# Attention's head mixings as float32 products in quarters of TensorE's array, two groups at once

## The chip, the cores and the metric

The kernel runs on one core of a Trainium2 chip. The metric is the device time of one execution in microseconds; before the change it is 1365.61 us, the median of three runs (1364.88 to 1365.74). Engines are named as in the profile: PE is the tensor engine (PEld its weight loads), DVE the vector engine, ACT the scalar engine, POOL GpSimd, SP the engine that issues most DMA transfers.

## The reference

```python
# q, k, v: (4, 12, 448, 64); w_pre, w_post: (12, 12)
scores = scale * np.matmul(q, k.transpose(0, 1, 3, 2))
scores = np.einsum('bhij,hg->bgij', scores, w_pre)      # premix over heads
scores = scores - np.max(scores, axis=-1, keepdims=True)
attn = np.exp(scores)
attn = attn / (np.sum(attn, axis=-1, keepdims=True) + 1e-09)
attn = np.einsum('bhij,hg->bgij', attn, w_post)          # postmix over heads
x = np.matmul(attn, v)                                   # then (1792, 768)
x = (sigmoid(x @ w_gate) * (x @ w_val)) @ w_out          # d_ff 1536
h = x @ w_in                                             # d_ff 2048
out = (h * sigmoid(1.702 * h)) @ w_out2                  # all in float32
```

Attention mixes its 12 heads twice with a 12 x 12 matrix: the scores before the softmax, and the weights after it.

## The kernel before, in words

The first part of the program is attention, the rest are the two feed-forward networks (class `Ffn`). A few of the feed-forward weights are loaded and prepared beside attention, and the feed-forward part's first matmuls (`pg`, L1005) stand among attention's last ones.

A unit is a batch and up to 120 query rows: 120, 120, 120 and 88 rows a batch, 16 units. For a unit, `qk` (L245) multiplies q and k for two heads at once, one on array rows 0 to 63 and one on rows 64 to 127, in three float32r passes over parts that were split high and low; `qk_out` copies the scores from PSUM to `sc`, with 120 query rows on partitions and head by column on the free axis. `relayout` (L266) moves ten of these rows by one DMA on SP into a tile `gt` whose partitions are (row, head), 10 x 12 = 120 of them. That is a group; there are 180. Then come, for each group,

- `split_hi` and `split_lo` (L214 and L278 in the trace): the scores are split into a high and a low float32r part, the cast on ACT or DVE, the subtraction on POOL or DVE;
- `premix` (L285): three float32r passes of 448 columns by a 120 x 120 block-diagonal weight, itself split (`wphl`), into one PSUM bank;
- `rowmax` (L292, DVE), `expo` (L299, ACT, which also sums each row);
- `norm` (L307, L309 on DVE, L312 on ACT): one over the sum, and the block-diagonal `wpost` scaled by it into `w2`;
- `postmix` (L330): four plain float32 matmuls whose stationary side is 112 columns of exp and whose moving side is `w2`, so the result comes out with keys on partitions; the trace counts two passes for each float32 matmul;
- `post_out` (L214, to `at`): the copy out of PSUM, on ACT or DVE.

When a unit's groups are through, `av` (L349) multiplies `at` by v, two heads at once on the two column halves of the array, and `av_out` and `store` bring it to DRAM.

The order of all this on each engine is made when the program is built, by `Work`: every piece has a due time (a group every `STEP` = 2350), a cost on each engine that may run it, what it needs, and which buffers it takes and gives back. `order()` picks piece by piece the one that can begin first. PSUM stands there as two pools: four single banks `s` (for transposes of the first batch, premix, postmix, A·V) and two double banks `q` (q·k, and later transposes). Engines run their lists strictly in that order.

## Time and profile before

| | us |
|---|---|
| median of three runs | 1365.61 |
| span of the profiled execution | 1370.6 |
| PE busy over the span | 1342.6 (98%) |
| DVE busy | 1097.7 (80%) |
| ACT busy | 913.1 (67%) |
| POOL busy | 173.7 (13%) |

The profiled execution's own time is its span. Busy time of PE counts each pass from its start to its modelled end, and passes overlap, so a busy PE need not issue at its peak; how far apart passes start is read from runs of equal passes. POOL works only in the first 12 of the profile's 40 slices, which is attention.

### The profile page before, as it was taken

How to read it: one execution, taken by the hardware profiler on the slowest of the kernel's cores; microseconds unless marked ns; L12 is line 12 of the kernel's file. 1: busy time of each engine (PE TensorE's matmuls, PEld its weight loads, DVE VectorE, ACT ScalarE, POOL GpSimd, SP SyncE). 2: the span in 40 equal slices, each digit the busy share in tenths (PEclk: the TensorE clock that was granted, in tenths of full speed). 3: DMA queues.
4: the chain of work that ended last, by engine and by line, in shares of the span. 5: the costliest groups of instructions: out<-in, count | busy, mean ns of one | idle time of the engine just before them, and what ended most of it. 6: DMA issues, size and time to landing. Idle time of an engine off the chain costs nothing.

```text
span 1370.6 us, 26095 instructions
## 1 busy us (share of the span) xinstructions
PE 1342.6 (98%) x8862; PEld 1230.6 (90%) x8862; DVE 1097.7 (80%) x2534; ACT 913.1 (67%) x2162; POOL 173.7 (13%) x160
## 2 busy tenths in 40 slices
PE   7999999999999999999999999999999999999998
PEld 5888888888888999998999889998999998999998
DVE  5888878898889889989988988877875697665763
ACT  5888978888888756776765766565666364565442
POOL 2443433344442000000000000000000000000000
PEclk9999999999999999999999999999999999999999
DMA  5655755744455665557997645586752875214644
GB/s 148 193 163 163 225 168 155 224 159 159 158 180 182 224 220 162 172 177 251 309 306 265 209 158 170 195 278 224 232 166 82 251 245 175 69 41 141 208 141 136
DMA packets 224148, 256.40 MB, mean 187 GB/s; under 512 B 70268, under 2 KB 211472, under 8 KB 224016
## 3 DMA queue, kind: packets, MB, share of 16 engines
q1 hardware_dynamic: 222992, 254.50, 58.3%
q8 instruction: 70, 1.15, 0.4%
q14 instruction: 62, 0.51, 0.1%
q10 hardware_dynamic: 960, 0.23, 0.1%
q0 software_dynamic: 64, 0.01, 0.0%
HBM read 160.18 MB, written 55.97 MB: 158 GB/s over the span
## 4 chain that ended last, share of the span: by engine, by line
PE 46%; DVE 7%; DMA 5%; issue 2%; ACT 2%; SPq 0%; DVEq 0%; ACTq 0%
PE pq L1060 25%; PE po L1547 15%; PE py L1005 5%; DMA ws<-in_moe_w_in_dram 3%; DVE w L927 2%; DMA sb<-xy 1%; DVE xy L1042 1%; DVE wc L802 1%; DVE s L1198 1%; DVE wc L804 1%; DVE wc L801 1%; DVE s L1069 1%; DMA xy<-kept 0%; DMA kept<-wc 0%; ACT xy L1041 0%
## 5 line engine op out<-in xcount | busy, mean ns | idle before, releaser
L1060 PE MATMUL pq<-xy,w 128*128 128x448 f32 x2394 | 482.7, 363 | 3.9 <-ACT w L921 1.0
L1060 PEld LDWEIGHTS pq<-xy,w 128*128 128x128 f32 x2394 | 447.9, 188 | 38.1 <-ACT w L921 2.6
L1547 PE MATMUL po<-wf,xy 128*128 128x384 f32 x1176 | 208.5, 338 | 3.1 <-ACT xy L993 1.6
L1547 PEld LDWEIGHTS po<-wf,xy 128*128 128x128 f32 x1176 | 207.6, 188 | 3.8 <-ACT xy L993 1.9
L278 POOL TENSOR_TENSOR ghl<-gt,ghl 120x448 fp32r<-120x448 f32 (+1 forms) x144 | 168.9, 1179 | 243.1 <-ACT ghl L214 176.9
L330 PEld LDWEIGHTS pso<-w,ex 120*112 120x112 f32 (+1 forms) x1440 | 160.3, 177 | 22.6 <-ACT ex L299 6.9
L330 PE MATMUL pso<-w,ex 120*112 120x120 f32 (+1 forms) x1440 | 173.3, 270 | 3.3 <-ACT ex L299 1.5
L1005 PE MATMUL py<-xy,w 128*128 128x448 f32 x864 | 173.7, 362 | 1.5 <-DVE xy L991 1.4
L1005 PEld LDWEIGHTS py<-xy,w 128*128 128x128 f32 x864 | 162.0, 188 | 12.8 <-DVE xy L991 2.1
L285 PE MATMUL psp<-ghl,wphl 120*120 120x448 f32 x540 | 141.8, 388 | 1.9 <-ACT ex L299 1.4
L1041 ACT CAST xy<-xy 128x384 fp32r<-128x384 f32 (+2 forms) x212 | 89.2, 457 | 59.3 <-DVE xy L1198 56.3
L292 DVE TENSOR_REDUCE st<-psp 120x1 f32<-120x448 f32 x180 | 108.8, 613 | 13.6 <-PE psp L285 13.4
L299 ACT ACTIVATE ex<-psp,st 120x448 f32<-120x448 f32 x180 | 113.6, 635 | 7.3 <-DVE st L292 2.8
L1042 DVE TENSOR_TENSOR xy<-xy 128x384 fp32r<-128x384 f32 (+2 forms) x212 | 95.9, 487 | 23.4 <-ACT xy L1041 23.3
L285 PEld LDWEIGHTS psp<-ghl,wphl 120*120 120x120 f32 x540 | 89.5, 184 | 17.4 <-ACT ex L299 3.9
L1198 DVE TENSOR_TENSOR xy<-xy 128x384 f32<-128x384 f32 (+2 forms) x184 | 91.0, 512 | 16.9 <-DMA xy<-xd 7.4
L921 ACT CAST w<-xy 128x384 fp32r<-128x384 f32 x110 | 55.2, 511 | 53.9 <-DVE xy L1198 32.1
L214 ACT CAST ghl<-gt 120x448 fp32r<-120x448 f32 (+1 forms) x135 | 75.7, 566 | 17.3 <-PE psp L285 12.0
L927 DVE TENSOR_TENSOR w<-wt,w 128x384 fp32r<-128x384 f32 x108 | 59.3, 554 | 27.7 <-ACT w L921 27.6
L798 ACT ACTIVATE wc<-ws 128x384 f32<-128x384 f32 x108 | 59.8, 554 | 32.2 <-DMA ws<-in_moe_w_in_dram 23.2
L245 PE MATMUL psq<-kq 64*120 64x448 f32 (+1 forms) x576 | 75.1, 392 | 3.7 <-ACT sc L214 3.1
L349 PEld LDWEIGHTS psv<-at,vt 112*64 112x64 f32 x1536 | 73.7, 137 | 5.2 <-issue 1.3
(96 smaller groups left out, 1793.1 us busy)
## 6 DMA issues: line engine op xcount, KB each, us to landing
gt<-sc SPq DMA_DIRECT2D x172, 210.0 KB
wf<-sb SPq DMA_DIRECT2D x64, 384.0 KB
xy<-kept SPq DMA_DIRECT2D x60, 384.0 KB
ws<-in_moe_w_out_dram SPq DMA_DIRECT2D x56, 384.0 KB
kept<-wc SPq DMA_DIRECT2D x108, 192.0 KB
ws<-kept SPq DMA_DIRECT2D x46, 384.0 KB
sb<-xy SPq DMA_DIRECT2D x32, 384.0 KB
ws<-in_moe_w_in_dram SPq DMA_DIRECT2D x32, 384.0 KB
```

Source lines behind the costliest of these rows:

```text
L278: eng.tensor_tensor(out=t[:m, 1], in0=gt.pop(s)[:m], in1=t[:m, 0].bitcast(F32), op=ALU.subtract)
L285: nc.tensor.matmul(ps[:m, :S], wphl[:m, wp, :m], t[:m, gp], start=(i == 0), stop=(i == 2))
L292: nc.vector.tensor_reduce(out=st[:m, 0:1], in_=pre[s][:m, :S], axis=AX.X, op=ALU.max, negate=True)
L299: nc.scalar.activation(t[:m], pre.pop(s)[:m, :S], AF.Exp, bias=st[:m, 0:1], scale=1.0, accum_out=st[:m, 1:2])
L330: nc.tensor.matmul(ps[:JC, c, :, :n], e[:m, c * JC:(c + 1) * JC], w[:m, :, :n], start=True, stop=True)
L927: self.nc.vector.tensor_tensor(out=w[:, 1], in0=self.source(i), in1=w[:, 0].bitcast(F32), op=ALU.subtract)
L1005: self.nc.tensor.matmul(acc[hb][:, :self.S], st, act[k0 + kc][hb][:, ap], start=(k0 + kc == 0 and part == 0 and ap == 0), stop=(k0 + kc == ...
L1041: self.nc.scalar.copy(dst[:, 0], src)
L1042: self.after(n, lambda: self.nc.vector.tensor_tensor(out=dst[:, 1], in0=src, in1=dst[:, 0].bitcast(F32), op=ALU.subtract))
L1060: nc.tensor.matmul(x, st, A[p][c][:, ap], start=(first and c + part + ap == 0), stop=(c == self.KG - 1 and part == 1), skip_group_check=no ...
L1198: self.nc.vector.tensor_tensor(out=dst, in0=x, in1=y, op=op)
L1547: nc.tensor.matmul(acc[:, :PW], x[:, part], w[:, wp], start=(start and part == 0 and wp == 0), stop=(stop and part == 1), skip_group_check ...
```

## The change

The heads are mixed in quarters of the array. A group now holds four blocks of five (or four) rows: 5 x 12 = 60 partitions fit one half of the array, and two blocks lie on partitions 4 to 63 and 64 to 123 of `gts`, two more beside them on the free axis. `premix` is four plain float32 matmuls of 64 x 64 by 448 columns, one in each quarter, into two banks (one for each row half). `postmix` is 32 float32 matmuls: for each of four key chunks and two blocks on the free axis, two column halves of keys (64 and 48) by two row halves. A unit of 120 rows has six such groups, one of 88 rows five (two of 20 rows, three of 16): 92 in all. The scores are no longer split, so `split_hi`, `split_lo` and `split_w` are gone, and the premix waits for the two DMAs of its group directly. Scaling `w2` moves from ACT to POOL, for both blocks at once. `rowmax`, `expo` and `post_out` run twice a group. The score buffers `gts` are five fixed tiles whose first 32 partitions POOL clears once; `build_w` builds each weight in two halves.

PSUM is now eight single banks which `Work` hands out by number: a piece asks for `banks`, and each copy out `frees` one. Four of them (`kept`) outlive attention; pieces marked `late` (the last unit's) use those alone. `STEP` is 3600, and buffers for exp and `w2` are five of the double size instead of eight. The due times of the feed-forward weights prepared beside attention are multiplied by 0.72.

```diff
-    IG = 10
-    CI = 12 * IG
+    IG = 5
+    CI = 120
+    NR = IG * H
...
-    SL = 2
-    EB = 8
+    EB = 5
...
-        ps_s = ctx.enter_context(tc.tile_pool(name="ps_s", bufs=SB, space=PSUM))
-        ps_q = early.enter_context(tc.tile_pool(name="ps_q", bufs=2, space=PSUM, side="right"))
-
-        wphl = const.tile([CI, 2, CI], F32R, name="wphl")
-        wpre = const.tile([CI, CI], F32, name="wpre")
-        wpost = const.tile([CI, H, IG], F32, name="wpost")
+        bank = [pool.enter_context(tc.tile_pool(name=f"bank{i}", bufs=1, space=PSUM, side=side)).tile([128, 512], F32, name=f"bank{i}")
+                for pool, side, some in ((ctx, "left", range(SB)), (early, "right", range(SB, 8))) for i in some]
+        now = {}
...
+        wpre = const.tile([128, 64], F32, name="wpre")
+        wpost = const.tile([128, H, IG], F32, name="wpost")
+        gts = [const.tile([128, 2, S], F32, name=f"gt{i}") for i in range(PF + 1)]
...
+            for x in (wpre, wpost, *(x[:32] for x in gts)):
+                nc.gpsimd.memset(x, 0.0)
...
+                for half in range(2):
+                    off = 64 - NR if (i, half) == (0, 0) else 0
+                    p0 = 64 * half + off
+                    nc.gpsimd.dma_start(rep[p0:p0 + NR], src.unsqueeze(0).broadcast_to([IG, H, H]))
...
-        def relayout(s):
-            u, g, count, m = groups[s]
-            t = g_p.tile([CI, S], F32, tag="g", name="gt")
-            nc.sync.dma_start(t[:m * H], sc[u][g:g + (m - 1) * count + 1:count])
-            gt[s] = t
-
-        def split_hi(s, eng):
-            m = groups[s][3] * H
-            t = g_p.tile([CI, 2, S], F32R, tag="ghl", name="ghl", bufs=SL + 1)
-            copy(eng, t[:m, 0], gt[s][:m])
-            ghl[s] = t
-
-        def split_lo(s, eng):
-            m = groups[s][3] * H
-            t = ghl[s]
-            eng.tensor_tensor(out=t[:m, 1], in0=gt.pop(s)[:m], in1=t[:m, 0].bitcast(F32), op=ALU.subtract)
+        def relayout(s, j):
+
+            u, g, r0, x, count, m = groups[s]
+            r0 += x + j
+            nc.sync.dma_start(gts[s % len(gts)][64 - m * H:64 + m * H, j], sc[u][r0:r0 + (2 * m - 1) * count + 1:count])
 
         def premix(s):
-            m = groups[s][3] * H
-            ps = ps_s.tile([128, 512], F32, tag="s", name="psp")
-            t = ghl.pop(s)
-            for i, (wp, gp) in enumerate(((0, 0), (1, 0), (0, 1))):
...
+            m = groups[s][-1]
+            x = gts[s % len(gts)]
+            pre[s] = banks_of(now["x"])
+            for col in range(2):
+                for row, r in enumerate((slice(0, 64), slice(64, 64 + m * H))):
+                    nc.tensor.matmul(pre[s][row][64 * col:64 * col + 64, :S], wpre[r], x[r, col], start=True, stop=True,
+                                     tile_position=(64 * row, 64 * col))
+
...
+        def expo(s, j):
+            if j == 0:
+                ex[s] = e_p.tile([128, 2, S], F32, tag="e", name="ex")
             st = rs[s]
-            nc.scalar.activation(t[:m], pre.pop(s)[:m, :S], AF.Exp, bias=st[:m, 0:1], scale=1.0,
-                                 accum_out=st[:m, 1:2])
-            ex[s] = t
+            nc.scalar.activation(ex[s][:, j], pre[s][j][:, :S], AF.Exp, bias=st[:, j:j + 1], scale=1.0,
+                                 accum_out=st[:, 2 + j:3 + j])
+            if j:
+                del pre[s]
...
-                w2[s] = w2_p.tile([CI, H, IG], F32, tag="w2", name="w2")
-                nc.scalar.activation(w2[s][:m], wpost[:m], AF.Copy, scale=r)
+                w2[s] = w2_p.tile([128, 2, NR], F32, tag="w2", name="w2")
+                nc.gpsimd.tensor_tensor(out=w2[s], in0=wpost.rearrange("p g i -> p (g i)").unsqueeze(1).broadcast_to([128, 2, NR]),
+                                        in1=r.unsqueeze(2).broadcast_to([128, 2, NR]), op=ALU.mult)
...
         def postmix(s):
-            u, g, count, n = groups[s]
-            m = n * H
+
+            u, m = groups[s][0], groups[s][-1]
             if u not in at:
                 at[u] = a_p.tile([JC, NJ, H, CI], F32, tag="a", name="at")
-            ps = ps_s.tile([128, NJ, H, IG], F32, tag="s", name="pso")
+            ps = [x[:, :NJ * H * 2 * IG].rearrange("p (c g i) -> p c g i", c=NJ, g=H) for x in banks_of(now["x"])]
             e = ex.pop(s)
-            w = w2.pop(s)
+            w = w2.pop(s).rearrange("p j (g i) -> p j g i", g=H)
             for c in range(NJ):
-                nc.tensor.matmul(ps[:JC, c, :, :n], e[:m, c * JC:(c + 1) * JC], w[:m, :, :n],
-                                 start=True, stop=True)
+                for j in range(2):
+                    i0 = IG - m if j == 0 else 0
+                    for k in (slice(0, 64), slice(64, JC)):
+                        for row in range(2):
+                            r = slice(64 * row, 64 * row + (i0 + m) * H)
+                            nc.tensor.matmul(ps[row][k, c, :, j * m:(j + 1) * m], e[r, j, c * JC + k.start:c * JC + k.stop],
+                                             w[r, j, :, i0:i0 + m], start=True, stop=True, tile_position=(64 * row, k.start))
...
+            re = []
+            for j in range(2):
+                re.append(work.add(t - PF * STEP + j, dict(SP=(820, 5000 if s < PF else 3500)), lambda e, j=j: relayout(s, j),
+                                   needs=made[u], takes=() if j else ("g",), behind=re[:1]))
+            moved.setdefault(u, []).extend(re)
+            pm = work.add(t, dict(PE=(800, 970)), lambda e: premix(s), needs=re, banks=2, late=s >= TAIL, gives=("g",), mode="quad")
+            xs = []
+            for j in range(2):
+                mx = work.add(t + 1000 + 600 * j, dict(DVE=(530, 615)), lambda e, j=j: rowmax(s, j), needs=[pm],
+                              takes=() if j else ("st",), behind=xs[:1])
+                xp = work.add(t + 1700 + 800 * j, dict(ACT=(830, 920)), lambda e, j=j: expo(s, j), needs=[mx],
+                              takes=() if j else ("e",), frees=((pm, j),), behind=xs[1:])
+                xs = [mx, xp]
+            n0 = work.add(t + 3500, dict(DVE=(75, 190)), lambda e: norm(s, 0), needs=xs[1:])
+            n1 = work.add(t + 3600, dict(DVE=(80, 190)), lambda e: norm(s, 1), needs=[n0])
+            n2 = work.add(t + 3700, dict(POOL=(450, 800)), lambda e: norm(s, 2), needs=[n1], takes=("w2",), gives=("st",))
+            po = work.add(t + 5400, dict(PE=(1000, 1170)), lambda e: postmix(s), needs=[n2],
+                          takes=("a",) if g == 0 else (), banks=2, late=s >= TAIL, gives=("e", "w2"), mode="quad")
...
```

On PE, in the middle of attention, a stretch of the list before reads (`psp` is a premix, `pso` a postmix, `psq` q·k; a matmul's result stands left of the arrow; x3 is three in a row):

```order
L330 MATMUL pso_4095<-w2_4021,ex_4002 112x120 x4
L330 MATMUL pso_4107<-w2_4036,ex_4026 112x120 x4
L285 MATMUL psp_4115<-ghl_3942,wphl_255 120x448 x3
L330 MATMUL pso_4122<-w2_4076,ex_4058 112x120 x4
L285 MATMUL psp_4135<-ghl_4009,wphl_255 120x448 x3
L285 MATMUL psp_4142<-ghl_4051,wphl_255 120x448 x3
L285 MATMUL psp_4152<-ghl_4127,wphl_255 120x448 x3
L245 MATMUL psq_4167<-kq_1838 120x448 x6
L245 MATMUL psq_4174<-kq_2859 120x448 x6
```

and after, from one premix to the start of the next postmix:

```order
L302 MATMUL bank6_273<-gt0_280,wpre_278 64x448
L302 MATMUL bank4_265<-gt0_280,wpre_278 64x448
L302 MATMUL bank6_273<-gt0_280,wpre_278 64x448
L302 MATMUL bank4_265<-gt0_280,wpre_278 64x448
L239 MATMUL bank3_261<-ident_285,nat_2074 128x112 x4
L239 MATMUL bank1_253<-ident_285,nat_2074 128x112 x4
L351 MATMUL bank0_249<-w2_3241,ex_3224 64x12x5
L351 MATMUL bank2_257<-w2_3241,ex_3224 64x12x5
L351 MATMUL bank0_249<-w2_3241,ex_3224 48x12x5
L351 MATMUL bank2_257<-w2_3241,ex_3224 48x12x5
L351 MATMUL bank0_249<-w2_3241,ex_3224 64x12x5
L351 MATMUL bank2_257<-w2_3241,ex_3224 64x12x5
```

A group's premix has gone from three passes of the whole array into one bank to four quarter matmuls that alternate between two banks; the postmix that begins at the end goes on for 32 matmuls, alternating between its two banks and between 64 and 48 keys.

On ACT, a stretch of the list before (`ghl` is the high part of the split scores, `w2` the scaled weight, `ex` exp, `at` the postmix's copy out, `sc` that of q·k):

```order
L312 ACTIVATE w2_2967<-wpost_257,st_2911 120x120
L299 ACTIVATE ex_2970,st_2955<-psp_2930,st_2955 120x448
L214 COPY at_2739<-pso_2959 112x48x10
L299 ACTIVATE ex_2995,st_2972<-psp_2937,st_2972 120x448
L299 ACTIVATE ex_3000,st_2993<-psp_2948,st_2993 120x448
L312 ACTIVATE w2_3013<-wpost_257,st_2955 120x120
L214 COPY sc_2974<-psq_2982 88x448
L312 ACTIVATE w2_3023<-wpost_257,st_2972 120x120
L214 COPY sc_2974<-psq_2975 88x448
L214 CAST ghl_3034<-gt_2924 120x448
```

and after:

```order
L243 COPY at_4609<-bank5_269 112x48x10
L243 COPY at_4609<-bank1_253 112x48x10
L314 ACTIVATE ex_4728,st_4724<-bank6_273,st_4724 128x448
L314 ACTIVATE ex_4728,st_4724<-bank7_277,st_4724 128x448
L314 ACTIVATE ex_4761,st_4744<-bank5_269,st_4744 128x448
L314 ACTIVATE ex_4761,st_4744<-bank2_257,st_4744 128x448
L314 ACTIVATE ex_4777,st_4765<-bank1_253,st_4765 128x448
L314 ACTIVATE ex_4777,st_4765<-bank0_249,st_4765 128x448
```

The casts to `ghl` and the scalings of `w2` have left ACT; two exps of one group follow each other, from two banks, into one tile.

On POOL, with what each instruction waits for, the list before repeats one subtraction a group, behind ACT's or DVE's cast; after, it repeats one scaling a group, behind DVE's norm and, from the sixth on, PE's postmix that frees the buffer (the names are counters of those engines):

```order
L278 TENSOR_TENSOR ghl<-gt,ghl 120x448 [waits DMAHW2_49,Activation_49]
L278 TENSOR_TENSOR ghl<-gt,ghl 120x448 [waits DMAHW4_49,Activation_49]
L278 TENSOR_TENSOR ghl<-gt,ghl 120x448 [waits DMAHW6_49,DVE_49,PE_49]
L278 TENSOR_TENSOR ghl<-gt,ghl 120x448 [waits DMAHW0_49,Activation_49]
L278 TENSOR_TENSOR ghl<-gt,ghl 120x448 [waits DMAHW1_49,DVE_49,PE_49]
```

```order
L207 TENSOR_SCALAR wpre_278<-wpre_278 128x64 [waits Pool_49]
L327 TENSOR_TENSOR w2_567<-wpost_279,st_539 128x120 [waits DVE_49,Activation_49]
L327 TENSOR_TENSOR w2_626<-wpost_279,st_550 128x120 [waits DVE_49,Activation_49]
L327 TENSOR_TENSOR w2_690<-wpost_279,st_582 128x120 [waits DVE_49,Activation_49]
L327 TENSOR_TENSOR w2_755<-wpost_279,st_680 128x120 [waits DVE_49,Activation_49]
L327 TENSOR_TENSOR w2_767<-wpost_279,st_693 128x120 [waits DVE_49,Activation_49]
L327 TENSOR_TENSOR w2_853<-wpost_279,st_730 128x120 [waits PE_49,DVE_49,Activation_49,Pool_49]
```

So POOL stood ahead of the premix and held a score buffer until its subtraction was done; it now stands between the norm and the postmix.

## Rows read from the trace of the kernel before

**Rows 1.** Two stages of the span: busy time and instructions of each engine, granted clock, DMA.
```profile
core 0: us, PE busy (x) PEld busy (x) DVE busy (x) ACT busy (x) POOL busy (x), PEclk, DMA share, GB/s
...
30.00:460.00 430.00, 422.83 (x4049) 366.05 (x4048) 374.38 (x990) 362.30 (x947) 166.83 (x143) 1.00 0.58 180
...
495.00:1370.00 875.00, 863.47 (x4434) 817.07 (x4433) 684.97 (x1459) 520.19 (x1152) 0.00 (x0) 1.00 0.59 192
```

**Rows 2.** Matmuls of premix and A·V: durations (min/median/max), first and last start.
```profile
L285 PE MATMUL psp<-ghl,wphl x540: 358/367/727, 30.2 to 459.4; 120*120 120x448 f32 x172, 108*108 108x448 f32 x8
...
L349 PE MATMUL psv<-at,vt x1536: 238/266/318, 54.0 to 470.5; 112*64 112x120 f32 x144, 112*64 112x88 f32 x48
```

**Rows 3.** Who PE's weight loads waited for, 30 to 450 us: total, times, longest.
```profile
PEld pso L330 <- ACT ex L299: 6.9, 16, 1.2
PEld pso L330 <- ACT w L312: 4.5, 13, 0.8
```

**Rows 4.** Timeline of PE: start, length; q·k, postmix, A·V.
```profile
203.58 0.98 PE L330 MATMUL pso<-w,ex 120*112 120x120 f32 x8
205.11 1.46 PE L245 MATMUL psq<-kq 64*88 64x448 f32 x12
...
195.42 5.14 PE L349 MATMUL psv<-at,vt 112*64 112x120 f32 x96
```

**Rows 5.** Groups by line and form, 0 to 470 us; the first row is the whole span's.
```profile
L1060 PE MATMUL pq<-xy,w 128*128 128x448 f32 x2394 | 482.7, 363 | 3.9 <-ACT w L921 1.0
...
L330 PE MATMUL pso<-w,ex 120*112 120x120 f32 x1376 | 166.1, 270 | 3.3 <-ACT ex L299 1.5 <-ACT w L312 0.4 <-DVE xo L368 0.4
L330 PEld LDWEIGHTS pso<-w,ex 120*112 120x112 f32 x1376 | 153.4, 177 | 21.8 <-ACT ex L299 6.6 <-ACT w L312 4.5 <-issue 4.1
L349 PEld LDWEIGHTS psv<-at,vt 112*64 112x64 f32 x1523 | 73.2, 137 | 5.2 <-issue 1.3 <-ACT at L214 1.0 <-DVE at L214 0.6
L330 PE MATMUL pso<-w,ex 108*112 108x108 f32 x64 | 7.6, 264 | 0.0
...
L299 ACT ACTIVATE ex<-psp,st 120x448 f32<-120x448 f32 x172 | 108.6, 635 | 7.3 <-DVE st L292 2.8 <-DVE st L309 1.8 <-DVE st L307 0.7
L299 ACT ACTIVATION_READ_ACCUMULATOR ex<-psp,st 120x1 f32 x172 | 34.7, 202 | 0.0
L214 ACT CAST ghl<-gt 120x448 fp32r<-120x448 f32 x128 | 71.9, 566 | 17.3 <-PE psp L285 12.0 <-DMA gt<-sc 4.4
L312 ACT ACTIVATE w<-wpost,st 120x120 f32<-120x120 f32 x172 | 66.3, 398 | 11.9 <-DVE st L309 8.0 <-DVE st L307 3.3
L278 POOL TENSOR_TENSOR ghl<-gt,ghl 120x448 fp32r<-120x448 f32 x140 | 164.3, 1179 | 223.9 <-ACT ghl L214 160.9 <-PE pso L330 13.9 <-DVE ghl L214 11.2
L214 DVE CAST ghl<-gt 120x448 fp32r<-120x448 f32 x44 | 25.9, 588 | 2.4 <-POOL ghl L278 1.6 <-DMA gt<-sc 0.8
L278 DVE TENSOR_TENSOR ghl<-gt,ghl 120x448 fp32r<-120x448 f32 x32 | 25.4, 793 | 1.8 <-ACT ghl L214 1.8
L278 DVE TENSOR_TENSOR ghl<-gt,ghl 108x448 fp32r<-108x448 f32 x4 | 2.9, 714 | 0.0
L309 DVE RECIPROCAL st<-st 120x1 f32<-120x1 f32 x172 | 25.4, 152 | 0.7
L307 DVE TENSOR_SCALAR st<-st 120x1 f32<-120x1 f32 x172 | 23.9, 143 | 10.0 <-ACT ex L299 9.6
```

**Rows 6.** SP's queue: a wait in 30 to 460 us, and two score moves issued.
```profile
SPq L266 <- POOL ghl L278: 72.6, 82, 4.9
...
104.03 1.74 SPq L266 DMA_DIRECT2D gt<-sc  x2
```

**Rows 7.** Timeline of POOL at the start: the first mixing weight.
```profile
1.64 0.73 POOL L163 DMA_DIRECT2D rep<-in_w_pre_dram  x1
4.90 0.28 POOL L164 COPY wpre<-rep 120x120 f32<-120x120 f32 x1 [2.54 <-DMA rep<-in_w_pre_dram]
5.25 0.76 POOL L168 TENSOR_SCALAR_AFFINE_SELECT wpre<-wpre 120x120 f32<-120x120 f32 x2
```

More of the change, by code (lines that the diff above doesn't have):

```diff
@@ L33, in __init__, with add, room @@
         self.pieces = []
-    def add(self, due, engines, emit, needs=(), takes=(), gives=(), mode=None, behind=(), since=0.0):
+        self.open = {x: 0.0 for x in range(banks)}
+        self.kept = kept
+    def add(self, due, engines, emit, needs=(), takes=(), gives=(), mode=None, behind=(), since=0.0, banks=0, frees=(),
+            late=False):
         self.pieces.append(dict(due=due, engines=engines, emit=emit, needs=list(needs), takes=takes, gives=gives,
                                 mode=mode, behind=list(behind), since=since, begin=None, i=len(self.pieces),
-                                end=None))
+                                end=None, wants=banks, frees=frees, late=late, banks=None))
         return self.pieces[-1]
+    def room(self, x):
+        return sorted((t, b) for b, t in self.open.items() if b < self.kept or not x["late"])[:x["wants"]]
     def order(self):
@@ L72, in order @@
                 self.free[p].append(x["end"])
+            for y, n in x["frees"]:
+                self.open[y["banks"][n]] = x["end"]
             open_.remove(x)
@@ L125, in attention @@
     last = {}
-    for s, (u, g, count, _) in enumerate(groups):
+    for s, (u, g, *_) in enumerate(groups):
         first.setdefault(u, s)
@@ L443, in add_scores @@
                     made.setdefault(u, []).append(y)
-                    prev = [y]
+                    in_banks.append(y)
         def add_group(s):
-            u, g, count, n = groups[s]
-            end = g == last[u]
+            u, g = groups[s][:2]
             t = s * STEP
-            re = work.add(t - PF * STEP, dict(SP=(900, 5000 if s <= PF else 3400)), lambda e: relayout(s), needs=made[u], takes=("g",))
-            moved.setdefault(u, []).append(re)
-            hi = work.add(t - 2 * STEP, dict(ACT=(470, 580), DVE=(740, 830)), lambda e: split_hi(s, e),
-                          needs=[re], takes=("ghl",))
@@ L454, in add_group @@
-            both = dict(POOL=(1150, 1250)) if s < ng - LATE else {}
-            lo = work.add(t - 2 * STEP + 400, dict(**both, DVE=(530, 620)), lambda e: split_lo(s, e),
-                          needs=[hi], gives=("g",))
-            pm = work.add(t, dict(PE=(610, 780)), lambda e: premix(s), needs=[lo], takes=("s",), gives=("ghl",))
-            mx = work.add(t + 700, dict(DVE=(522, 610)), lambda e: rowmax(s), needs=[pm], takes=("st",))
-            xp = work.add(t + 1300, dict(ACT=(624, 740)), lambda e: expo(s), needs=[mx], takes=("e",), gives=("s",))
@@ L469, in add_group @@
                 begun[u] = po
-            ao = work.add(t + 4300, dict(ACT=(460, 580), DVE=(565, 660)), lambda e: post_out(s, e), needs=[po],
-                          gives=("s",))
-            out.setdefault(u, []).append(ao)
+            prev = []
+            for row in range(2):
+                prev = [work.add(t + 6600 + 300 * row, dict(ACT=(490, 610), DVE=(565, 660)),
+                                 lambda e, row=row: post_out(s, row, e), needs=[po], behind=prev, frees=((po, row),))]
+                out.setdefault(u, []).append(prev[0])
+                if s < TAIL:
+                    in_banks.append(prev[0])
         def add_av(u):
@@ L477, in add_av @@
             x = work.add(t, dict(PE=(40.8 * n + 200, 40.8 * n + 365)), lambda e: av(u),
-                         needs=out[u] + [vready[b, c] for c in range(4)], takes=("s", "s"), mode="columns",
+                         needs=out[u] + [vready[b, c] for c in range(4)], banks=2, late=first[u] + last[u] + 1 >= TAIL, mode="columns",
                          gives=("a", "v") if u % nu == nu - 1 else ("a",))
@@ L482, in add_av @@
                 prev = [work.add(t + half * STEP + 900, dict(DVE=(650, 800)), lambda e, half=half: av_out(u, half),
[L483 removed]
+                                 needs=[x] + prev, takes=() if half else ("xo",), frees=((x, half),))]
+                if first[u] + last[u] + 1 < TAIL:
+                    in_banks.append(prev[0])
             stored[u] = work.add(t + 2 * STEP, dict(SP=(700, 3500)), lambda e: store(u), needs=prev, gives=("xo",))
```

182 lines of the change are left out of this document (87 added, 95 removed).

## The prediction

> **What bounds the kernel now.** I first cut the span into stages [rows 1]. Attention is the stage from 30 us to about 470 us: the first premix matmul starts at 30.2 us and the last A·V matmul at 470.5 us [rows 2]. What follows is the two feed-forward networks; the change touches none of their operations, so only attention can become shorter. In 30 to 460 us the tensor engine (PE) is busy 422.83 of 430 us, 98%, at the full granted clock (1.00), while VectorE (DVE) has 374.38, ScalarE (ACT) 362.30 and GpSimd (POOL) 166.83 us [rows 1]. Then I asked who keeps PE waiting: its longest entries are its weight loads behind ACT's exp (6.9 us in 16 waits) and behind ACT's scaled w (4.5 us) [rows 3]. So PE sets the pace, with DVE at 87% and ACT at 84% close behind. The profiled span of 1370.6 us is 5.0 us (0.4%) above the median of the runs, 1365.61; I make the sum as a difference within the profiled execution and take it off the median unchanged.
>
> **PE's work per 20 rows, before.** Two groups of ten query rows. A float32r pass of 448 columns costs 0.202 us when it runs back to back (482.7 us for 2394 of them [rows 5]), so a premix of three passes is 0.605 us. A postmix is eight passes in 0.98 us, the last of which takes 0.270 us to its end [rows 4, 5]: (0.98 - 0.27)/7 = 0.101 us each, 0.81 us for eight. A group is 1.42 us, 20 rows 2.83 us, and the 180 groups 255 us.
>
> **PE's work per 20 rows, after.** Float32 needs two passes a matmul (the postmix of four matmuls is x8 in the trace), and a pass of 120 columns costs 0.101 us, so 0.84 ns a column. The premix is four quarters of 448 columns: if all four run abreast, 2 x 448 x 0.84 = 0.75 us, taken as 0.80 for their offset starts. The postmix is 32 matmuls, 64 passes of 60 (or 48) columns, 16 deep if four run abreast. A pass streams 60 x 0.84 = 50 ns. The weight load grows from 137 ns for 64 columns to 177 ns for 112 [rows 5], 0.83 ns a column, so it needs 53 ns for 64 columns: the load and not the stream is the longer one. 16 x 53 = 0.85 us; with offsets I take 0.95. Together 1.75 us. Each batch has 23 such double groups (six, six, six and five), so there are 92: 161 us. PE loses 255 - 161 = 94 us of work.
>
> Is "abreast" shown? Two abreast is. The 96 passes of A·V, on the two column halves, take 5.14 us [rows 4]: (5.14 - 0.27)/95 = 51 ns each, half of the 101 ns that a 120-column pass takes alone. The twelve passes of a q·k pair, on the two row halves, take 1.46 us [rows 4], 0.10 us each after taking off the last one's end, half of 0.202. Both cuts at once stand in no row. The bounds for a double group are therefore 1.75 us (four abreast) and, two abreast, 4 x 2 x 0.376/2 + 64 x 0.053/2 = 1.50 + 1.70 = 3.20 us. I take four abreast, because each cut alone gave its whole factor of two.
>
> The new output runs are five elements of every ten in a PSUM bank. The nearest row has runs of nine of ten: 264 ns against 270 ns for whole runs, with 108 columns against 120 [rows 5], and 12 columns less are worth 10 ns by the 0.84 ns above. So gaps cost at most 4 ns there. The Trainium skill, "PSUM — Partial Sum Buffer", section Specifications, speaks against the change here: it says that any non-contiguous access pattern in PSUM slows matmuls significantly, and gives no figure. The row does not bear it out for gaps of one element; runs of five no row shows. If they doubled a pass, a postmix would be 1.6 us, as in the third rival below.
>
> **DVE, ACT, POOL and SP.** The splits go: on DVE 44 + 1 casts and 36 subtractions, 25.9 + 25.4 + 2.9 = 54 us, and half of the two small norm steps, (25.4 + 23.9)/2 = 25 us; 79 us in all [rows 5]. Over 440 us DVE had 383; 304 remain, and 2 us for four more row maxima. ACT loses 71.9 us of split casts and 66.3 us of weight scaling [rows 5], of 371: some 233 remain. Exp keeps its 635 + 202 ns; it runs over 128 partitions instead of 120. POOL loses the subtractions (164.3 us) and gets 92 multiplications of 128 x 120. The bounds are 0.28 us (its copy of 120 elements, [rows 7]) and 1.18 us (its tensor_tensor of 448 [rows 5]); I take 0.5, so 46 us, off the path: POOL is then under 15% busy, and five double groups of exp and w2 buffers lie between its result and the postmix. If that cover is gone, the chain of each group is a few tenths longer, which is in the range below. SP issues 184 moves of scores instead of 180, the same 21504 rows; one takes 0.87 us (1.74 for two), so 160 us [rows 6]. Its queue waited 72.6 us for POOL's subtraction to free a score buffer [rows 6]; this wait ends, and the premix itself now frees the buffer. Behind a waiting move stand the loads of q, k and v of the next batch, and PE's transposes wait for those.
>
> At the start POOL clears five score buffers and builds both weights in halves. One weight now takes from 1.64 us (its load's issue) to 6.01 us (the end of its masking) [rows 7], 4.4 us; four halves at that price, one behind the other, and about 6 us of clearing end near 23 us. The first premix stood at 30.2 us and shouldn't move up by more than these 7 us; I count nothing.
>
> **The sum.** From 30.2 to 470.5 us is 440 us; at 98% PE has 433 us of work there, after the change 433 - 94 = 339. How much of the 94 arrives depends on how well PE is fed. At 98% as now: 339/0.98 = 346, a gain of 94. At 87%, the share that DVE reaches while it waits on others: 390, a gain of 50. PE is still the busiest (DVE 306 us, 82% of 373), but the margin is as thin as before, while a piece is twice as large: two banks stay taken from a premix until two exps are through, and a postmix waits for the second exp, two norm steps and POOL. I take 0.91: 339/0.91 = 373, a gain of 67 us, and 1365.6 - 67 = **1299 us**.
>
> **Rivals.**
> - *PE is fed as now.* The gain is the full 94 us: 1272. For it: ACT falls from 84% to 62% and nothing new is near 90%. Against it: the longer chain per piece.
> - *The queue between the engines becomes the limit.* If ACT, DVE, the banks or SP's moves leave PE only 80%: 339/0.80 = 424, a gain of 16: 1350. For it: two banks a piece, and in the order the premix now hangs directly on two moves. Against it: each of these engines loses work or keeps it.
> - *Small passes don't issue fast enough.* The closest spacing of passes in any row is the 51 ns of A·V. If 64 passes of 60 columns can't come closer than half of that, 26 ns, a postmix is 1.64 us, a double group 2.44, 92 of them 224: PE then has 433 - 31 = 402 us, at 0.96 419: a gain of 21, 1345. The Trainium skill, "TensorEngine Tiling (Array Packing)", section Instruction Overhead, has such a rule: each matmul carries about 60 cycles, and a dimension that is already small should not be tiled. By it, at the 2.4 GHz of the granted 1.00, I estimate 25 ns a pass and 1.6 us a postmix, so the time of this rival. No row here has passes short enough to show it.
> - *Quarters run only two abreast.* 92 x 3.20 = 294 us, 39 more than before: PE has 472 us, at 0.98 482, 42 us longer: 1408. It decides from the point where a double group costs more than 2.83 us. Against it: both cuts show their factor of two; for it: never both together.
>
> **How the numbers follow.** Within 0.2%, 2.7 us, a measurement of this kernel can't be told from no change. The forecast, 1280 to 1325, gets 0.60; the gain nearer to the full 94 us, 0.14; the two rivals that leave 16 to 21 us, with all between them and the forecast, 0.14; no change 0.03; slower, two abreast above all, 0.09. So faster is 0.60 + 0.14 + 0.14 = 0.88. The range goes from 1268 (a little beyond the full 94) to 1345 and leaves out no change, slower, and part of the weak gains.
>
> **What would show it.** Premix groups of eight passes with about 0.95 us from the first start to the last end, and postmix groups of 64 passes with about 1.1 us, show four abreast; 1.7 and 1.9 us show two. The last A·V matmul should stand near 403 us, and from there to the end the time should be what it is now, 900 us. POOL's multiplication should read 0.4 to 0.8 us. DVE should be near 80% busy from 30 to 390 us, ACT near 60%. The prediction is wrong if PE's waits behind exp and POOL come to more than 70 us there, if the postmix is above 1.5 us, or if the feed-forward part changes its length.

## The result and the profile after

| | median us | runs, us |
|---|---|---|
| before | 1365.67 | 4, 1364.88 to 1369.2 |
| after | 1325.25 | 4, 1323.45 to 1330.61 |

The ratio is 0.9704, 95% interval 0.9682 to 0.9726: 40.4 us less, where the forecast had 67 us less and 1299. The sign, the mechanism and the range of 1268 to 1345 held; 26 us of the expected gain did not come. The time lies just outside the band of 1280 to 1325 that had most of the chance.

Attention and what follows it, in the kernel after (busy time and instructions of each engine, granted clock, DMA share, GB/s), to compare with [rows 1]:

```profile
30.00:425.00 395.00, 359.74 (x8802) 263.82 (x8798) 314.81 (x762) 248.97 (x645) 35.69 (x91) 0.97 0.66 200
425.00:1323.00 898.00, 888.47 (x4566) 840.82 (x4562) 699.60 (x1488) 529.14 (x1170) 0.00 (x0) 1.00 0.59 193
```

The feed-forward part is 898 us long, as before (900). All that changed lies in attention. Against [rows 1], PE's share falls from 98 to 91% (359.74 of 395), its granted clock from 1.00 to 0.97, and the DMA share rises from 0.58 to 0.66: the same scores and loads go through a shorter phase.

Premix (L302), postmix (L351) and A·V (L372) by their source line (duration min/median/max, first and last start), to compare with [rows 2]:

```profile
L302 PE MATMUL bank<-gt,wpre x736: 532/536/1002, 22.7 to 411.9; 64*64 64x448 f32 x174, 60*64 60x448 f32 x6, 48*64 48x448 f32 x4
...
L351 PE MATMUL bank<-w,ex x5888: 199/218/356, 29.8 to 419.8; 60*48 60x60 f32 x91, 60*64 60x60 f32 x78, 48*48 48x48 f32 x8, 60*64 60x48 f32 x8
...
L372 PE MATMUL bank<-at,vt x1536: 239/266/462, 48.9 to 425.0; 112*64 112x120 f32 x144, 112*64 112x88 f32 x48
```

The last A·V matmul starts at 425.0 us, not at 470.5 [rows 2]; the forecast wanted 403. The first premix stands 7.5 us earlier.

The groups of instructions that the change touched, 30 to 425 us (busy, mean ns | idle before them, and what ended it), against [rows 5]:

```profile
L314 ACT ACTIVATE ex<-bank,st 128x448 f32<-128x448 f32 x179 | 112.1, 637 | 48.7 <-DVE st L308 48.3
L351 PE MATMUL bank<-w,ex 60*64 60x60 f32 (+4 forms) x5888 | 111.4, 222 | 18.0 <-issue 7.9 <-POOL w L327 5.2 <-ACT at L243 1.8
L302 PE MATMUL bank<-gt,wpre 64*64 64x448 f32 (+2 forms) x712 | 108.5, 559 | 15.6 <-DMA gt<-sc 8.5 <-ACT ex L314 3.3 <-issue 2.6
...
L327 POOL TENSOR_TENSOR w<-wpost,st 128x120 f32<-128x120 f32 x91 | 35.7, 395 | 353.0 <-DVE st L324 184.7 <-ACT ex L314 123.5 <-ACT sc L243 12.8
```

The splits and ACT's scaling of w are gone; exp takes 637 ns as before, and POOL's multiplication 395 ns. ACT and DVE now stand idle for PE's results: exp, 48.7 us behind the row maxima, was at 7.3 us in [rows 5].

Whom PE's weight loads waited for, 24 to 400 us (total, times, longest), against [rows 3]:

```profile
PEld bank L351 <- issue: 23.5, 62, 1.8
PEld bank L302 <- DMA gt<-sc: 17.9, 20, 2.8
PEld bank L302 <- issue: 13.8, 41, 2.7
PEld bank L351 <- POOL w L327: 10.3, 11, 1.8
PEld bank L302 <- ACT ex L314: 8.2, 14, 2.0
```

The wait for gt, a score move that has not landed, is new. In the kernel before, the float32r split stood between the move and PE; now the premix hangs on the move itself.

What a late move does, in the weight loads' timeline (start, length): a premix of 20 rows is eight weight loads, four for each of its two moves. First one whose moves were both in, then one whose second move came late.

```profile
152.93 0.21 PEld L302 LDWEIGHTS bank<-gt,wpre 64*64 64x64 f32 x8 [0.31 <-issue]
...
223.93 0.22 PEld L302 LDWEIGHTS bank<-gt,wpre 64*64 64x64 f32 x4 [1.07 <-ACT sc L243]
224.69 0.20 PEld L302 LDWEIGHTS bank<-gt,wpre 64*64 64x64 f32 x4 [0.54 <-DMA gt<-sc]
```

The matmuls belonging to them, in PE's timeline:

```profile
152.93 0.98 PE L302 MATMUL bank<-gt,wpre 64*64 64x448 f32 x8
...
223.96 1.33 PE L302 MATMUL bank<-gt,wpre 64*64 64x448 f32 x6 [0.72 <-DMA gt<-sc]
224.80 0.43 PE L351 MATMUL bank<-w,ex 60*64 60x48 f32 x8
225.12 0.54 PE L302 MATMUL bank<-gt,wpre 64*64 64x448 f32 x2
```

With both moves in, four quarters run abreast: 0.98 us. With the second one late, the passes of the first column half run by themselves, two abreast, and those of the second after them: 223.96 to 225.66, 1.70 us. Eight passes of the next postmix (L351) begin beside it, so not all of this is lost. A late move thus costs PE by the wait and by the lost concurrency, and the second part counts as busy time. Of the 92 premix groups 29 took over 1.5 us: in 18 of them the fifth weight load waited for the second move; the others were held up by another engine, without a releaser, or by the lower clock told of below.

The third part is the granted clock. Three stretches around a late move, in which a premix stood from 93.3 to 95.33 us for its second half:

```profile
92.30:96.80 4.50, 2.43 (x12) 0.63 (x12) 0.42 (x4) 0.00 (x0) 0.00 (x0) 0.99 0.46 134
96.80:100.20 3.40, 3.40 (x12) 1.41 (x12) 2.29 (x5) 1.34 (x4) 0.39 (x1) 0.51 0.72 229
100.20:104.00 3.80, 3.54 (x87) 2.91 (x84) 3.02 (x10) 3.00 (x8) 0.39 (x1) 1.00 0.65 193
```

PE was busy 2.43 of 4.50 us, and then ran 3.4 us at 0.51 of the full clock, its lower level (1.2 GHz). Five such stretches, 20.5 us in all, lie in attention. In the kernel before there is one, from 26.7 to 33.6 us, at the start of the stage that [rows 1] gives as 1.00. The others in the kernel after follow waits of 1.0 to 2.6 us, for the norm step, for POOL, or without a releaser.

### The profile page after: what moved, and what is told of

Its sections match the earlier page's. It is cut to its first block, busy times and chain, and to the rows that moved or that the text cites. A ratio compares the mean times of both kernels' runs of the same rounds, so it can differ in the third digit from the quotient of the medians.

```text
span 1323.4 us, 34791 instructions
## 1 busy us (share of the span) xinstructions
PE 1270.7 (96%) x13506; PEld 1118.6 (85%) x13506; DVE 1032.6 (78%) x2289; ACT 793.5 (60%) x1849; POOL 47.4 (4%) x125
## 4 chain that ended last, share of the span: by engine, by line
PE 54%; DVE 5%; DMA 2%; issue 1%; ACT 1%; SPq 0%; DVEq 0%; ACTq 0%
PE pq L1085 27%; PE po L1572 15%; PE py L1030 12%; DVE w L952 1%; DMA xy<-kept 1%; DVE xy L1067 1%; DVE s L1223 1%; DMA sb<-xy 1%; DVE wc L827 1%; DVE s L1094 0%; DMA wf<-sb 0%; DVE xy L1223 0%; ACT xy L1066 0%; DVE wc L826 0%; DVE wc L829 0%
## 5 line engine op out<-in xcount | busy, mean ns | idle before, releaser
L314 ACT ACTIVATE ex<-bank,st 128x448 f32<-128x448 f32 x184 | 115.3, 637 | 50.4 <-DVE st L308 49.9
L351 PEld LDWEIGHTS bank<-w,ex 60*48 60x48 f32 (+2 forms) x5888 | 101.8, 131 | 44.2 <-issue 25.1
L351 PE MATMUL bank<-w,ex 60*64 60x60 f32 (+4 forms) x5888 | 111.4, 222 | 18.0 <-issue 7.9
L302 PE MATMUL bank<-gt,wpre 64*64 64x448 f32 (+2 forms) x736 | 112.6, 559 | 15.6 <-DMA gt<-sc 8.5
L308 DVE TENSOR_REDUCE st<-bank 128x1 f32<-128x448 f32 x184 | 108.2, 614 | 23.5 <-PE bank L302 22.5
L1223 DVE TENSOR_TENSOR xy<-xy 128x384 f32<-128x384 f32 (+2 forms) x184 | 90.7, 510 | 14.2 <-DMA xy<-xd 6.0
L372 PEld LDWEIGHTS bank<-at,vt 112*64 112x64 f32 x1536 | 75.5, 139 | 10.8 <-ACT ex L314 5.5
L372 PE MATMUL bank<-at,vt 112*64 112x120 f32 (+1 forms) x1536 | 78.9, 264 | 1.4 <-DVE at L243 0.9
L302 PEld LDWEIGHTS bank<-gt,wpre 64*64 64x64 f32 (+2 forms) x736 | 33.2, 134 | 54.1 <-DMA gt<-sc 18.1
L823 ACT ACTIVATE wc<-ws 128x384 f32<-128x384 f32 x108 | 59.7, 553 | 30.1 <-DMA ws<-in_moe_w_in_dram 22.2
L243 ACT COPY at<-bank 112x480 f32<-112x480 f32 (+1 forms) x91 | 49.6, 562 | 42.3 <-PE bank L351 41.0
L273 PE MATMUL bank<-kq 64*120 64x448 f32 (+1 forms) x576 | 72.8, 384 | 1.4 <-DVE kq L243 1.0
```

Of the source, the lines that this page charges most:

```text
L273: nc.tensor.matmul(ps[a][:n, :S], w[at_, qp, 1, i0:i0 + n], w[at_, kp, 0], start=(i == 0), stop=(i == 2), tile_position=(a * 64, 0))
L302: nc.tensor.matmul(pre[s][row][64 * col:64 * col + 64, :S], wpre[r], x[r, col], start=True, stop=True, tile_position=(64 * row, 64 * col))
L308: nc.vector.tensor_reduce(out=rs[s][:, j:j + 1], in_=pre[s][j][:, :S], axis=AX.X, op=ALU.max, negate=True)
L314: nc.scalar.activation(ex[s][:, j], pre[s][j][:, :S], AF.Exp, bias=st[:, j:j + 1], scale=1.0, accum_out=st[:, 2 + j:3 + j])
L351: nc.tensor.matmul(ps[row][k, c, :, j * m:(j + 1) * m], e[r, j, c * JC + k.start:c * JC + k.stop], w[r, j, :, i0:i0 + m], start=True, stop ...
L372: nc.tensor.matmul(ps[a * 64:a * 64 + 64, r, :n], vt[b][:, g, c, :], a_t[:, c, g, :n], start=(c == 0), stop=(c == NJ - 1), tile_position=( ...
```

## Experiments

Theory A: SyncE's queue, which issues in order, is too full (its instructions take 295 of 400 us; before, 269 of 446; added up from the trace). Theory B: transfers crowd each other, so that moves land late (issue to landing, worked out from the trace's packets: median 2.63 us before, 3.48 after; 90% within 3.78 and 5.69). Landing times of SyncE's moves are worked out in this way throughout, by taking the packets of a move's size in order. Also tried: instruction supply to PE, and the chain from exp to postmix. The ratios are to the kernel before, which ran beside each; it read 1367 to 1370 us there, so compare ratios. The other columns are PE's in the profiled run: busy time from 30 us to the last A·V start, the busy time of all premixes, and its waits for gt (matmuls and loads added). Loads and matmuls wait side by side, so the last column counts some time twice: in the kernel after, its 26.6 us cover 21.7 us, and the matmuls' own part is 8.5 us.

| kernel | median us | ratio, interval | last A·V | PE busy | premix | gt |
|---|---|---|---|---|---|---|
| after | 1325.25 | 0.9704, 0.9682–0.9726 | 425.0 | 359.7 | 112.6 | 26.6 |
| no moves | 1295.47 | 0.9469, 0.9434–0.9504 | 393.3 | 336.3 | 92.0 | 1.4 |
| one of two moves | 1300.32 | 0.9495, 0.9471–0.9520 | 398.3 | 343.6 | 95.3 | 1.5 |
| half rows | 1307.83 | 0.9541, 0.9513–0.9568 | 407.7 | 350.2 | 103.5 | 10.8 |
| small weight loads | 1312.00 | 0.9596, 0.9578–0.9613 | 410.3 | 351.3 | 108.3 | 18.6 |
| alternate | 1334.51 | 0.9757, 0.9723–0.9791 | 431.7 | 363.6 | 114.3 | 32.2 |
| no norm step | 1325.63 | 0.9689, 0.9656–0.9723 | 428.1 | 355.2 | 106.9 | 14.2 |
| late plan | 1332.64 | 0.9725, 0.9690–0.9761 | 435.0 | 358.7 | 104.0 | 20.7 |
| six buffers | 1341.14 | 0.9790, 0.9770–0.9810 | 441.0 | 360.8 | 114.3 | 27.9 |
| scaling on ACT | 1352.05 | 0.9865, 0.9838–0.9891 | 446.6 | 364.8 | 114.3 | 30.7 |
| six buffers, scaling on ACT | 1351.99 | 0.9865, 0.9834–0.9896 | 450.7 | 364.4 | 111.5 | 28.2 |
| half the moves by POOL | 1397.31 | 1.0208, 1.0170–1.0246 | 495.0 | 380.3 | 118.0 | 42.6 |

**Streams of passes on PE alone.** A kernel of its own, with no other engine's work in the way.

```diff
+        for i in range(40):
+            for c in range(4):
+                for half in range(2):
+                    for row in range(2):
...
+                        nc.tensor.matmul(view(2, row, k, 10, 5), e[...], w[r, :60]..., tile_position=(64 * row, 64 * half))
```

> Not the reference's computation: this kernel only streams float32 matmuls on PE and writes zeros as its output. Its stretches, each of 640 or 320 matmuls back to back: L58 quarters of 64x64 by 60 columns with output runs of five in ten; L66 the same with whole output runs; L74 quarters by 120 columns; L81 row halves of 112 columns by 60; L89 the premix's quarters by 448 columns; then, beside large loads, L58 and L89 again. Theory (PE's short passes outrun the fetching of its instructions): L58 stops about every 256 instructions for a few tenths of a microsecond to 1 us, so that 16 rounds of four passes take 1.1 to 1.5 us on average and not 0.93, and more beside the loads; L74, with half the instructions a microsecond, shows no stops and 0.10 us a round. Rival (the passes themselves are slow, and the stops in attention came from waits): L58 runs evenly, 0.93 us for 16 rounds or more, without stops at 256. Output runs of five in ten: no difference from L66 if gaps in a bank cost nothing. L89: 0.38 us a round if four run abreast, 0.75 if two do.

Its PE timeline: whole output runs (L66), a stream of 120 columns (L74), row halves (L81), and quarters of 448 columns (L88).

```profile
64.15 2.09 PE L66 MATMUL bank<-w,e 60*64 60x60 f32 x128 [1.37 <-issue]
67.88 2.09 PE L66 MATMUL bank<-w,e 60*64 60x60 f32 x128 [1.64 <-issue]
...
130.71 3.51 PE L74 MATMUL bank<-w,e 60*64 60x120 f32 x128 [0.22 <-issue]
...
137.05 31.68 PE L81 MATMUL bank<-w,e 60*112 60x60 f32 x640
168.66 9.25 PE L88 MATMUL bank<-e,w 64*64 64x448 f32 x96
```

Quarters do run four abreast: 96 passes of 448 columns in 9.25 us are 0.385 us for four. Short passes come in bursts of 128, 3.73 us apart, with a stop between them that waits for no engine: 128 passes and their 128 weight loads are 256 instructions, and in the trace one packet of the instruction queue ends at each stop; that PE waits there for its instructions is inferred from this. Within a burst four passes take 0.058 us, 14.5 ns each; over the stops it is 29 ns, or 1.86 us for 16 rounds of four, more than the 1.1 to 1.5 expected. Output in runs of five of ten takes the same 0.058. Beside loads of 419 GB/s the bursts stood 6.2 us apart (partly at the lower clock).

**Postmixes kept apart in the order.** If these stops were the loss, spreading the dense passes should bring it back.

```diff
- start = max(at, now.get(e, 0.0))
+ start = max(at, now.get(e, 0.0)) + (700 if e == "PE" and many and x.get("many") else 0)
```

> The order is made so that a postmix is put behind another postmix only where nothing else could begin within 0.7 us: 3 such pairs in place of 27. All work stays. Theory (instruction fetch stops PE where postmixes follow each other): the stops inside postmixes, some 10 to 12 us in attention, go, and the kernel takes 1313 to 1319 us. Rival (those stops are hidden behind other waits, or the new order waits elsewhere): 1322 to 1330 us.

(`many` marks a postmix.) PE's weight loads, 24 to 400 us:

```profile
PEld bank L354 <- issue: 30.1, 82, 4.3
```

It is 9 us slower than the kernel after (by the times; 7 by the ratios), outside both ranges expected. The postmix's waits without a releaser did not shrink (30.1 us against 23.5), and its waits for gt grew to 32.2 us. Counted over PE's passes and weight loads, most of the longer stops fall at the same place in a block of 256 instructions, here and in the kernel after, wherever the postmixes stand.

**Without the score moves.**

```diff
+ if s < len(gts):
      nc.sync.dma_start(gts[s % len(gts)][64 - m * H:64 + m * H, j], sc[u][...])
```

> Leaves out the score moves but for the first five groups: later groups mix the scores that already lie in the buffers, so the output is another. 174 of 184 moves on SP and PE's waits for them go, the order on every engine stays. Theory (late moves cost PE about 18 us of waiting, as the profile's waits say): 1303 to 1312 us. Rival (the wait only passes on to exp and the postmix's chain): 1319 to 1326 us. If the moves were all of the shortfall: 1298.

Its attention, 30 us to the last A·V, and its premix there:

```profile
30.00:393.30 363.30, 336.26 (x8806) 254.71 (x8802) 311.91 (x762) 249.73 (x646) 36.38 (x91) 1.00 0.42 118
```

```profile
L303 PE MATMUL bank<-gt,wpre 64*64 64x448 f32 (+1 forms) x712 | 87.9, 546 | 1.9 <-ACT ex L315 1.4 <-issue 0.5
```

1295.47: 30 us less, below every range expected, and close to the forecast. So the moves, with all that they hold up, cost about what the forecast missed; the edit also leaves more room to every other transfer (DMA share 0.42). Of the 31.7 us that the stretch is shorter (395.0 to 363.3), 23.5 are PE's busy time, and 20.6 of these its premixes (108.5 to 87.9); the other 8.2 are idle time. Six of 92 premixes now take over 1.5 us. The clock is at 1.00, with one stretch of 3.4 us at the lower level.

**Without the step that adds 1e-9.**

```diff
- n0 = work.add(t + 3500, dict(DVE=(75, 190)), lambda e: norm(s, 0), needs=xs[1:])
```

> Leaves out the addition of 1e-9 to the row sums (a sum holds exp(0) = 1, so float32 keeps it as it is). One DVE step of 0.16 us and its hand-over go out of the chain from the second exp to the postmix. Theory (the chain exp, norm, POOL is a third wait, some 10 us by the profile): 3 to 6 us less, 1319 to 1322 us. Rival (PE is held by moves and fetch, and the chain runs beside them): 1324 to 1327 us.

1325.63, the same as after: one link less in the chain from exp to postmix shows no gain. The order changed with it: the waits for gt came out lower (14.2 us), and yet the time stayed.

**Half rows; one move of two.** These split bytes from issues.

```diff
+ w = S if s < len(gts) else S // 2
+ nc.sync.dma_start(gts[...][..., j, :w], sc[u][..., :, :w])
```

> Every score move from the sixth double group on carries only the first half of each row (leaves out the other 224 of 448 columns, which keep an earlier group's scores); as many moves, each issued as before, in the same order. Theory A, SyncE's queue is what is short (it issues for some 295 of the 400 us of attention, 152 us of it moves, and the rest stands behind its waits): the time stays with the changed kernel, 1319 to 1327 us, and the waits of TensorE for gt stay above 20 us. Theory B, the transfers crowd each other (landing 3.5 us in place of 2.6): the time falls by half or more of what leaving the moves out gave, to 1299 to 1312 us.

```diff
+ if j == 0 or s < len(gts):
      nc.sync.dma_start(gts[...], sc[u][...])
```

> The second of each double group's two score moves is left out from the sixth group on (its half of the array works on an earlier group's scores); the order is unchanged. Theory A, SyncE's queue: some 76 us of issuing go, and it is no longer short: most of the 30 us comes back, 1296 to 1306 us. Theory B, crowded transfers: half of the bytes go, 1306 to 1314 us, the same as moves of half rows.

Half of the bytes with every issue kept gives 0.9704 - 0.9541 = 1.6% or 22 us; half of the bytes and half of the issues 29 us; no moves 32 us. Half rows land sooner (median 2.31 us, 90% within 3.31), though a group's last move is issued no earlier before its premix begins (7.0 us, 7.7 in the kernel after; medians from the sixth group on, from the trace): that is B. With one move of two, the moves land hardly sooner (3.10, 90% within 5.12), but the last one is issued 9.9 us ahead, the premix hangs on one move alone, and the wait for gt is gone; its time lies in the range that A had. So sooner landing and earlier issuing each bring back most of the loss, and the shares don't add up. Half of the issues with all the bytes was not run.

**Small weight loads, every move whole.** This takes other bytes away.

```diff
- st = pf.tile([128, self.PW, 2], U32, tag="pf", name="pf")
...
+ st = self.one
+ few = slice(0, 128 if i == self.pre[0] else 8)
- self.nc.sync.dma_start(st.rearrange(...), src)
+ self.nc.sync.dma_start(st.rearrange(...)[few], src[few])
```

> All score moves stay whole, and the order is unchanged; from the second of the 28 weight blocks on that are converted ahead during attention, the load fetches 8 of 128 partitions (leaves out the other 120, which keep the first block's values): some 9.7 MB less in flight, against some 18 MB less with moves of half rows. Theory B, transfers of any kind crowd the moves: the wait for gt falls from 26 us to 10 to 18 us and the time by about half of what half rows gave, to 1308 to 1317 us. Rival, what half rows saved lay in the moves' own length (a shorter move lands sooner whatever else is in flight): 1320 to 1328 us.

Waits for gt in this kernel, from 24 to 400 us, first the loads', then the matmuls':

```profile
PEld bank L302 <- DMA gt<-sc: 12.4, 17, 1.4
...
PE bank L302 <- DMA gt<-sc: 6.2, 9, 2.2
```

0.9596, 15 us less, as B expected; the wait for gt fell to 18.6 us, just above the 10 to 18 expected. The moves were untouched, and their median landing fell to 2.72 us: other transfers do delay them. But the late ones stay: 90% land within 5.01 us (5.69), 26 of 92 premixes still take over 1.5 us, and all premixes together are only 4.2 us shorter. The time at the lower clock fell from 20.5 to 6.8 us, and ACT's own waits for these loads from 26.3 to 11.0 us; how much of the 15 us came by the moves this run cannot separate.

**Five versions that compute everything, meant to be faster.** A plan that expects the moves later; half of the moves by GpSimd's queue; a sixth buffer of moved scores for a fifth of exponentials; the scaling of w back on ScalarE; and the last two together.

```diff
- dict(SP=(820, 5000 if s < PF else 3500))
+ dict(SP=(820, 5000 if s < PF else 5000))
```

> The plan that writes the order counts 5.0 us from a score move to its landing in place of 3.5 us; nothing else. If a large part of TensorE's waits comes from an order that expects the scores too early, 1312 to 1321 us, and the wait of the premixing passes for gt falls from 26 us to under 15 us. If the moves themselves are issued late (theory A) or land late in crowded stretches (B), the order cannot help: 1321 to 1330 us.

```diff
- nc.sync.dma_start(gts[...], sc[u][...])
+ (nc.gpsimd if j else nc.sync).dma_start(gts[...], sc[u][...])
...
- dict(SP=(820, 5000 if s < PF else 3500))
+ {("SP", "POOL")[j]: (820, 5000 if s < PF else 3500)}
```

> The second of each double group's two score moves is issued by GpSimd instead of SyncE (92 moves), and the plan's order is made for that; the bytes are the same. Theory A, SyncE's queue is short: 1300 to 1313 us, a version that beats the changed kernel. Theory B, crowded transfers: 1320 to 1330 us. Its own risk: GpSimd's move may take more than 1.5 us to issue and stand ahead of the scaling of the weights, which would make it 1330 to 1350 us.

Its moves as issued by POOL (last number: median us from issue to landing):

```profile
gt<-sc POOLq DMA_DIRECT2D x80, 210.0 KB, 6.4
```

A wait of POOL there, from 30 to 430 us:

```profile
POOL gt L293 <- PE bank L302: 33.7, 19, 6.6
```

```diff
- PF = 4
+ PF = 5
- EB = 5
+ EB = 4
```

> Six buffers for moved scores in place of five and four buffers of exponentials in place of five (the memory does not hold more); the plan issues each score move one double group earlier. The bytes are the same. Theory B (moves land late where transfers crowd each other, so that TensorE waits for gt): a lead of one group more, some 4 us, covers landings of up to 5.7 us, the wait of the premixing passes for gt falls from 18 us to under 8 us, and the time to 1305 to 1318 us. Rival, the crowd takes bandwidth that no lead gives back, or four buffers of exponentials hold back the row maxima: 1322 to 1335 us.

```diff
- nc.gpsimd.tensor_tensor(out=w2[s], in0=wpost..., in1=r..., op=ALU.mult)
+ for i in range(2): nc.scalar.activation(w2[s][:, i], wpost..., AF.Copy, scale=r[:, i:i + 1])
...
- dict(POOL=(450, 800))
+ dict(ACT=(580, 700))
```

> The scaling of the postmixing weights goes back from GpSimd to ScalarE, as two activations of one row each; the order is made for that (580 ns of ScalarE planned). Theory B says that this link is not what holds: the waits of the postmixing passes for GpSimd (10 us) become waits for ScalarE, 1320 to 1332 us. Rival, the chain from exponential to postmixing is a real part of the 27 us: 1312 to 1320 us.

> Both: six buffers of moved scores, four of exponentials, and the scaling on ScalarE. Theory B: as the six buffers alone, 1303 to 1318 us. Rival (four buffers of exponentials hold back): a shorter chain frees the exponentials earlier, so this one is at least 5 us below the six buffers alone, 1315 to 1328 us.

None beats the kernel after, and their times lie above every range expected. The late plan put 9.8 us between a group's last move and its premix and lowered the gt wait from 26.6 only to 20.7 us; by the ratios, which put it into its rival's range, it is 0.2% slower, within the intervals. With half of the moves on POOL the kernel is slower than before: POOL's moves need 6.4 us, SyncE's own now 6.0 (3.48 in the kernel after), and POOL, which does the scaling in the same list, stands 33.7 us until a premix frees the buffer for a move. The sixth buffer did not touch the wait for gt (27.9 us), but it gave no lead either: the last move is issued 7.7 us ahead of its premix, as in the kernel after, so lead is not tested by it. With the scaling on ACT the postmix waits for exp:

```profile
PEld bank L351 <- ACT ex L314: 19.5, 25, 4.1
...
PE bank L351 <- ACT ex L314: 10.1, 13, 3.3
```

That version is 22 us slower. The longer chain is the likely price, though a shorter one gave nothing; ACT's added work comes in the same edit. Both together: 1351.99, no better than the scaling alone. Each of these edits also rewrites the order; how much of their loss is the order itself was not separated.

## Why the prediction was right, and what it mis-sized

- *PE sets the pace, and its work shrinks by four abreast*: right. A premix group with both moves in takes 0.98 us, a postmix group 1.15 us from first start to last end, against 0.95 and 1.1 (medians of the 92: 1.05 and 1.15).
- *The rival "small passes don't issue fast enough"* fell: 14.5 ns a pass within a burst, under its 26. The Trainium skill, "TensorEngine Tiling (Array Packing)", section Instruction Overhead, states about 60 cycles a matmul, by which they were estimated at 25 ns; within a burst the measurement decides against it. Over long streams 29 ns a pass were measured, with the stops. In the kernel after, PE's waits without a releaser before postmix passes come to 7.9 us (L351 above); without the moves they are still 10.3 us.
- *Gaps in PSUM cost nothing*: right, 0.058 us for four passes either way. "PSUM — Partial Sum Buffer", section Specifications, of the Trainium skill warns against such patterns; no run here shows a price.
- *PE's share of 0.91*: over the phase that the sum means, from the first premix to the last A·V, it is 0.909 (365.66/402.30, first line below). The value had been picked between two bounds and not worked out, and it covers waits that the prediction did not have in mind; that it fits so well is in part luck.
- *PE's work of 339 us, with 0.80 us for every premix*: this step failed. It is 366 us, and 366/0.909 = 402, where the forecast had 373. Without moves (second line) PE is busy 341.81 of 370.23 us, nearly the forecast's 339 of 373.

```profile
22.70:425.00 402.30, 365.66 (x8842) 266.17 (x8840) 320.17 (x774) 253.03 (x657) 36.07 (x92) 0.97 0.66 201
```

```profile
23.07:393.30 370.23, 341.81 (x8842) 256.89 (x8840) 316.99 (x772) 253.46 (x656) 36.77 (x92) 1.00 0.43 120
```

The sum took every premix with both of its moves in; of the 92, 29 took over 1.5 us, 18 of them behind a late second move, and after some waits the clock was at its lower level. The prediction named the hazard ("in the order the premix now hangs directly on two moves") as a reason for its rival at 80%, 1350 us, and gave it no term in the sum; the measured time lies about half way to that rival.

- *SP: 184 moves, its wait for POOL ends*: the count was right, but a wait for the premix took its place (28.3 us), and neither how early a move is issued nor how long it takes to land was looked at. The DMA share of 0.58 in [rows 1] and the same bytes in 373 us in place of 440 give 0.68; 0.66 was measured. That number was there to be worked out.
- *Startup counts nothing*: it gave 7.5 us. So the phase from the first premix to the last A·V is 402 us against a forecast of 373, 29 more; 22 of that remain at its end. The feed-forward part came out 2 us shorter. Before's profiled span was 5.0 us above its median, after's is 1.9 us below its own. So 22 - 2 + 5 + 2 = 27 us did not come, the 26 of the result but for rounding.
- *DVE near 80%, ACT near 60%, POOL 0.4 to 0.8 us*: 80%, 63% (30 to 425 us), 0.395. None of the three signs of a wrong prediction came: the postmix's median stayed under 1.5 us, the feed-forward part kept its length, and PE's waits behind exp and POOL stayed under 70 us (43 us, matmuls and loads added, 24 to 425 us).

What stays open: how the loss by the moves divides between late issuing and slow landing, and between the wait, the halved premix and the clock. The clock's share can be bounded: 20.5 us at half of it are, as an estimate, at most 10 us of work, and with half rows just as long a time at the lower clock left the kernel 22 us faster. Whether another order of the loads would keep other transfers away from the moves was not tried.

## What to carry to other kernels

When an edit takes a step out between a transfer and the engine that sets the pace, that engine now waits for the transfer itself: look at how early it is issued and how long it takes to land, not only at the count of issues. A shorter phase with the same bytes has a higher DMA share; work it out beforehand. Where passes share the array, an operand that comes late costs the concurrency too, and the page shows that as busy time.

## What the hardware showed beyond that

- A stream of short matmuls on PE stops after each 256 instructions, weight loads counted: 128 passes in 2.09 us, then 1.6 us of nothing. Passes of 120 columns stop for 0.2 us in most places, and row halves of 49.5 ns a pass (31.68 us/640) not at all. The packets of the instruction queue:

```profile
q8 instruction: 106, 1.74, 0.5%
```

(packets, MB, share of 16 engines) in the kernel after; it was 70 before.
- With half of the score moves issued by GpSimd, its moves landed in 6.4 us and SyncE's in 6.0, where all of them on SyncE had landed in 3.48 (medians): the second issuer made neither kind land sooner.
